# Attention and mixture-of-experts kernel on one core: eight warming matmuls, other first loads, a second task order, and register loads moved behind copies

## The chip, the cores and the metric

The kernel runs on one core of one Trainium2 chip. The metric is the device time of the whole program in microseconds (us), lower is better. Before the change it is 468.69 us, the median of 3 runs (468.49 to 468.74).

## The reference, cut to what matters

The input is q, k, v of 4 batches, 8 heads, 576 rows, 64 columns, a memory per head, and the weights of 8 experts, all in float32.

```python
scores = where(causal, -1e9, q @ k.T / sqrt(64)); a = softmax(scores); local = a @ v
phi = where(x > 0, x, exp(x) - 1) + 1
mem_out = (phi(q) @ M_prev) / (phi(q) @ z_prev + 1e-6)
x = sigmoid(beta) * mem_out + (1 - sigmoid(beta)) * local      # 2304 rows of 512
e_idx = argmax(x @ w_gate, axis=1)
for e in range(8):                                             # each row goes to one expert
    out[e_idx == e] = gate_w * eom * (relu(x @ w1[e]) @ w2[e])
```

## The kernel before, in words

**Attention.** The 32 heads are handled as 16 pairs g = 0 to 15, four pairs to a batch. A pair's q and k lie transposed in one tile `qk` (128 partitions, 1280 columns): 64 columns of q's last rows (`TQ`), then the q block, then k. Each value is split into a rounded part `hi` and the remainder `lo` (float32r), and a score block is three matmuls: hi by lo, lo by hi, hi by hi (`score`, L549). The first operand named is the stationary one and comes from q, the second from k.

A step is a pair and one of five row blocks qt. Its tasks are: SS (scores, TensorE), M (mask, scale and row minimum, VectorE, L628 and L596), E (exponential, ScalarE, L633), T (transposes, TensorE, L645), V (copy of the transposed block out of PSUM, ScalarE or VectorE, L492). Per pair there are also load and load_v (transfers, issued by SyncE), C (`hi` of a whole pair, ScalarE, L461), R (`lo` of a whole pair, GpSimd, L465), P (values, TensorE, L680), O (copy of P's result), and F0 to F2 (phi of q). Per batch there are MW and MC (memory weights), ME, N1, N2, G (memory term), PV, Y, XD, OUT (sum of both terms and its store), LT to LA (logits), RT, RK, Tgate, Tpos, SEL (routing). The last batch uses PL, YL, TL, XL instead of PV, Y and XD. Z tasks and fetch prepare the fullest expert early.

**The order of the work.** The list `ORDER` (L50) names all 1181 tasks of the attention; a loop (L1092) emits them one by one. Each engine executes its own instructions strictly in that order, so `ORDER` fixes the queue of every engine. A name with `:ACT` or `:DVE` behind it is a copy that can go to either engine.

**The start.** `warm(12)` (L941) issues twelve bf16 matmuls of 512 columns on a tile of ones, which TensorE executes while the first transfers run. `load(0)` (L429) brings pair 0 in pieces (`pieces`, L411): k columns and q columns of the first 256 rows (128 KB each), then k (160 KB) and q (192 KB) of the other rows, then TQ (32 KB). The first q piece is issued by ScalarE's queue, all others by SyncE's. `load(1)` (640 KB, L953) follows. Then `first(0)` and `first_low(0)` (L467, L474) make `hi` and `lo` of the first pieces: VectorE casts k, ScalarE casts q, VectorE subtracts q and then k. `constants()` (L194) issues the transfers of beta, wg and rzt. Tasks first1 to first3 repeat this for the second pieces: ScalarE and VectorE cast, VectorE subtracts q, GpSimd subtracts k.

**The experts.** After the attention the rows are gathered expert by expert in 17 slots of 128 rows. `gemm1` (L1441) multiplies a slot by w1, `stage_h` (L1448) transposes the result on TensorE and makes hT and hh on ScalarE and hl = hT - hh on GpSimd, and `gemm2` (L1468) multiplies by w2. A function given to `gemm1` as `mid` is emitted in the middle of its matmuls. `numbers(g0, g1)` (L1545) loads expert numbers from the tile `groupi` into ScalarE's registers; `wide_load` (L1549) uses them for the addresses of transfers that ScalarE issues. Between the experts' set-up and the slot loop stand these lines:

```python
1639    numbers(0, QUARTERS)                 # three registers
1640    gemm1(1, lambda: stage_h(0))
```

Of the kernel before, what the change touches and what calls it, by code (L numbers as in the profile page):

```python
# [54 lines left out]
T1_2_0 V1_2_0:ACT T1_2_1 M2_0_0 M2_0_1 M2_1_1 E2_0_1 TS0_0 F03 P0_256_0 V1_2_1:DVE E2_0_0 E2_1_1 T1_4 M1_3_1 F21 V1_4_0:ACT LM1 M2_1_0 M1_3_0 P0_256_1
C3:DVE F12 P1_0_0 E2_1_0 V1_4_1:DVE T2_0 load4 E1_3_0 E1_3_1 V2_0:DVE SS2_2 R3 M2_2_0 M2_2_1 O0_256:ACT O1_0:ACT SS2_3 T2_1 T1_3_1 load_v3 E2_2_0
V2_1:ACT M2_3_0 V1_3_1:ACT TS1_0 E2_3_0 SS2_4 T1_3_0 V1_3_0:ACT M2_3_1 MW1 F13 F04 E2_2_1 T2_2_0 T2_3_0 TS1_1 ranks M2_4_0 P1_256_0 C4:DVE E2_3_1 F22 MC1
V2_2_0:ACT SS3_1 M3_0_0 V2_3_0:ACT P1_256_1 T2_2_1 M3_1_0 M2_4_1 E2_4 V2_2_1:ACT E3_0_0 load5 F23 O1_256:DVE M3_0_1 T2_3_1 TS2_0 load6 E3_0_1 E3_1_0
V2_3_1:DVE SS3_2 ME0_0 M3_2_1 T2_4 E3_2_1 R4 M3_1_1 wgz V2_4_0:ACT N10_0 N20_0 V2_4_1:ACT F06 SS3_4 T3_2_1 T3_0 M3_2_0 ME0_1 F14 V3_0:ACT M3_4_0
V3_2_1:ACT SS4_1 M3_4_1 E3_2_0 N10_1 SS4_2 E3_1_1 N20_1 T3_1 T3_2_0 C5:ACT P2_0_0 P2_256_0 TS2_1 E3_4 M4_0_0 V3_1:ACT M4_0_1 F24 M4_2_1 G0_1 M4_2_0  # L60
V3_2_0:ACT O2_0:ACT E4_0_1 E4_0_0 T3_4 M4_1_1 E4_1_1 E4_2_1 P2_256_1 V3_4_0:DVE TS3_0 M4_1_0 O2_256:DVE T4_0 SS3_3 E4_1_0 load_v4 E4_2_0 V3_4_1:DVE
M3_3_0 ME0_4 C6:ACT V4_0:ACT T4_2_0 SS4_4 V4_2_0:ACT R5 N10_4 T4_2_1 R6 TS3_1 N20_4 M3_3_1 M4_4_0 V4_2_1:ACT T4_1 E3_3_0 M4_4_1 load7 E3_3_1 V4_1:ACT
ME0_3 SS4_3 E4_4 T3_3_1 V3_3_1:ACT T3_3_0 N10_3 V3_3_0:ACT N20_3 M4_3_0 F16 E4_3_0 M4_3_1 ME0_2 N10_2 TS4_0 F05 SS5_1 SS5_2 N20_2 F26 T4_4 M5_0_0
M5_0_1 E4_3_1 P3_0_0 V4_4_0:DVE P3_256_0 O3_0:ACT E5_0_0 load9 P4_0_0 E5_0_1 M5_1_0 G0_3 P3_256_1 load_v5 F15 C7:ACT M5_2_0 W0 O3_256:ACT T4_3_0
O4_0:ACT F07 V4_4_1:DVE F25 E5_1_0 R7 T4_3_1 PV0_2 M5_2_1 M5_1_1 PV0_1 SS5_4 V4_3_1:ACT E5_1_1 E5_2_1 V4_3_0:DVE T5_0 Y0_2 G0_4 V5_0:ACT E5_2_0 Y0_1
M5_4_0 SS5_3 G0_0 M5_4_1 LT0_0 load8 XD0_1 LC0_0:DVE T5_2_0 V5_2_0:ACT XD0_2 M5_3_1 T5_1 PV0_4 E5_4 M5_3_0 T5_2_1 SS6_2 SS6_1 V5_2_1:DVE F09 V5_1:ACT
E5_3_0 E5_3_1 Y0_4 OUT0_2 M6_0_0 LT0_1 F08 M6_2_1 LC0_1:ACT T5_4 load_v7 OUT0_1 E6_0_0 V5_4_0:ACT F19 M6_2_0 LM2 LS0 SS6_4 TS5_1 V5_4_1:ACT TS5_0
E6_2_1 F17 M6_1_0 TS4_1 T5_3_1 T5_3_0 LY0 XD0_4 M6_0_1 E6_0_1 LB0 G0_2 V5_3_1:ACT V5_3_0:ACT PV0_0 P4_256_0 M6_1_1 T6_2_1 F18 LA0 RT0_0 Y0_0 E6_1_1
E6_1_0 RT0_1 T6_0 SS7_1 XD0_0 P4_256_1 P5_256_0 O4_256:ACT V6_0:ACT V6_2_1:DVE M6_4_0 RT0_2 E6_2_0 C8:ACT R8 F27 RT0_3 RT0_4 M7_0_0 P5_0_0 P5_256_1
OUT0_4 T6_1 CA0 F28 E7_0_0 O5_0:ACT M6_4_1 E6_4 O5_256:DVE T6_2_0 load_v6 V6_2_0:ACT M7_0_1 M7_1_1 ME1_0 SS6_3 M7_1_0 SS7_3 load_v8 V6_1:ACT load10  # L70
E7_1_1 RX0 N11_0 E7_0_1 C9:ACT T6_4 N21_0 V6_4_0:ACT E7_1_0 PV0_3 M6_3_1 E6_3_1 M6_3_0 P6_0_0 Y0_3 V6_4_1:DVE TS6_0 E6_3_0 T7_0 O6_0:DVE M7_3_0 M7_3_1
R9 TS6_1 V7_0:ACT SS7_2 ME1_4 N11_4 E7_3_0 T6_3_1 T7_1 E7_3_1 SS7_4 V7_1:ACT N21_4 M7_2_0 Tgate10 E7_2_0 V6_3_1:ACT M7_2_1 ME1_2 G1_0 N11_2 SS8_1
T6_3_0 N21_2 F29 Tgate30 T7_3_1 V6_3_0:ACT V7_3_1:ACT C10:ACT MW2 MC2 M7_4_0 T7_3_0 M8_0_0 OUT0_0 E7_2_1 M8_0_1 load11 M7_4_1 ME1_1 XD0_3 T7_2_1 N11_1
N21_1 V7_3_0:ACT T7_2_0 E8_0_0 R10 SS8_2 E7_4 M8_1_1 ME1_3 M8_1_0 V7_2_1:ACT V7_2_0:ACT E8_0_1 E8_1_1 M8_2_0 Tgate20 F011 T7_4 OUT0_3 load13 SS8_3
# [16 lines left out]
P11_256_1 M12_4_1 SEL1_2 T12_1 M13_0_0 T12_3_1 M13_1_0 O11_256:ACT M13_0_1 V12_1:ACT M13_1_1 E12_4 XD2_1 PV2_4 PV2_3 R14 Y2_4 E13_1_1 T12_3_0 E13_0_1
SS12_2 SS13_3 XD2_4 OUT2_1 OUT2_4 V12_3_1:ACT V12_3_0:DVE M12_2_1 G2_4 E13_1_0 GA1 E13_0_0 T12_4 Y2_3 V12_4_0:ACT E12_2_1 F014 LT2_0 M12_2_0 LT2_1
T13_0 F012 SEL1_1 XD2_3 V12_4_1:DVE T13_1 LC2_0:DVE LC2_1:ACT V13_0:DVE M13_3_0 LS2 E12_2_0 V13_1:ACT SS13_2 T12_2_0 T12_2_1 E13_3_0 V12_2_1:ACT LY2
P12_0_0 M13_3_1 TS12_0 SEL0_4 load_v13 V12_2_0:ACT M13_2_0 O12_0:ACT PV2_0 LB2 M13_2_1 E13_2_0 SS13_4 T13_3_0 PV2_2 Y2_0 F112 F114 T13_2_0 Y2_2
# [1709 lines left out]
```

## Time and profile before

| what | value |
|---|---|
| median of 3 runs | 468.69 us (468.49 to 468.74) |
| the profiled execution's own time | 468.34 us |
| its span, first to last instruction | 466.3 us |
| instructions | 10798 |
| TensorE busy | 456.7 us (98% of the span) |
| VectorE, ScalarE, GpSimd busy | 284.9, 262.4, 271.1 us |

The span is what the trace covers; the profiled execution's own time is 2.0 us longer. A busy TensorE is not a TensorE at its peak, since a matmul that is held up counts as busy while it is pipelined. In the trace PE is TensorE's matmuls, PEld its weight loads, DVE VectorE, ACT ScalarE, POOL GpSimd, SP SyncE, and a q behind a name is that engine's sequencer, which issues transfers. An idle stretch in square brackets is followed by what ended it.

### The profile page before, as it was taken

What the parts mean: (1) busy time and instruction counts of PE and PEld (TensorE: products, weight loads), DVE (VectorE), ACT (ScalarE), POOL (GpSimd) and SP (SyncE); (2) the same over time, 40 slices, a digit from 0 to 9 for tenths busy, and PEclk for the clock granted to TensorE, in tenths of its full rate; (3) what the DMA queues carried; (4) which work ended last, traced back from release to release, by engine and by line L of the source; (5) the groups of instructions that cost most, each with busy time, mean ns of one, the idle gap of its engine ahead of it and who ended that gap; (6) DMA issues with size and microseconds to landing.
All of it is one profiled execution on the core that took longest, in us unless ns stands there. A gap on an engine that the chain in (4) does not pass through costs nothing.

```text
span 466.3 us, 10798 instructions
## 1 busy us (share of the span) xinstructions
PE 456.7 (98%) x3517; PEld 354.8 (76%) x3517; DVE 284.9 (61%) x851; ACT 262.4 (56%) x625; POOL 271.1 (58%) x274
## 2 busy tenths in 40 slices
...
GB/s 239 204 144 143 21 216 158 158 58 199 30 153 30 86 181 99 59 142 153 47 265 324 299 309 170 328 46 346 265 202 341 115 208 221 124 147 182 29 31 39
DMA packets 30119, 75.90 MB, mean 163 GB/s; under 512 B 4307, under 2 KB 4839, under 8 KB 30058
## 3 DMA queue, kind: packets, MB, share of 16 engines
...
## 4 chain that ended last, share of the span: by engine, by line
PE 88%; DVE 3%; issue 2%; POOL 2%; ACT 2%; DVEq 1%; POOLq 0%; ACTq 0%
PE py L1432 18%; PE h L1432 17%; PE po L680 10%; PE pt L645 8%; PE s L570 7%; PE me L736 4%; PE hp L1458 3%; PE cy L1601 3%; PE ch L1601 3%; PE sd L557 3%; PE pt L614 2%; PE px L1400 2%; PE he L1123 1%; PE pv L799 1%; PE pl L904 1%
## 5 line engine op out<-in xcount | busy, mean ns | idle before, releaser
L633 ACT ACTIVATE st<-st,nm 128x128 f32<-128x128 f32 (+3 forms) x128 | 71.4, 562 | 3.7 <-DVE nm L628 3.6
L1465 POOL TENSOR_TENSOR hl<-hT,hh 128x512 fp32r<-128x512 f32 x32 | 43.5, 1380 | 40.6 <-ACT hh L1464 40.5
L628 DVE CUSTOM_DVE_ANT_0 st<-s,mask 128x128 f32<-128x128 f32 (+3 forms) x128 | 58.2, 483 | 8.2 <-PE s L570 4.1
L1108 DVE CAST whi<-kept 128x1024 fp32r<-128x1024 f32 x32 | 26.0, 811 | 51.6 <-ACTq L1439 40.7
L465 POOL TENSOR_TENSOR lo<-qk,hi 128x1216 fp32r<-128x1216 f32 x15 | 42.1, 2805 | 24.7 <-ACT hi L461 19.5
L1111 DVE TENSOR_TENSOR wlo<-kept,whi 128x1024 fp32r<-128x1024 f32 x32 | 54.4, 1701 | 1.1
L492 ACT COPY PT<-pt 128x512 f32<-128x512 f32 (+2 forms) x89 | 45.2, 523 | 15.9 <-PE pt L645 13.8
L1432 PE MATMUL h<-whi,xh 128*128 (+1 forms) x136 | 53.9, 396 | 0.0
L1432 PE MATMUL h<-whi,xl 128*128 (+1 forms) x136 | 53.4, 393 | 0.0
L1432 PE MATMUL h<-wlo,xh 128*128 (+1 forms) x136 | 53.4, 392 | 0.0
L1432 PE MATMUL py<-whi,hh 128*128 (+1 forms) x128 | 51.9, 406 | 0.0
L1432 PE MATMUL py<-whi,hl 128*128 (+1 forms) x128 | 50.2, 392 | 0.3 <-POOL hl L1465 0.3
L1432 PE MATMUL py<-wlo,hh 128*128 (+1 forms) x128 | 50.2, 392 | 0.0
L680 PE MATMUL po<-PT,v 128*64 128x320 f32 (+4 forms) x480 | 49.1, 349 | 0.8 <-ACT oT_hT L492 0.4
L645 PE MATMUL pt<-ident,st 128*128 128x128 f32 x320 | 48.0, 280 | 0.4 <-ACT st L633 0.4
L1464 ACT CAST hh<-hp 128x512 fp32r<-128x512 f32 x32 | 19.1, 598 | 50.6 <-PE py L1432 50.6
L1445 ACT ACTIVATE h<-h 128x1024 f32<-128x1024 f32 x17 | 17.5, 1029 | 47.9 <-PE h L1432 47.9
L680 PEld LDWEIGHTS po<-PT,v 128*64 128x64 f32 x480 | 29.6, 137 | 17.7 <-issue 2.8
L1411 POOL TENSOR_TENSOR xl<-x,xh 128x512 fp32r<-128x512 f32 x16 | 21.7, 1358 | 34.3 <-issue 19.0
L645 PEld LDWEIGHTS pt<-ident,st 128*128 128x128 f32 x320 | 35.2, 142 | 7.8 <-ACT st L633 2.5
...
L1432 PEld LDWEIGHTS h<-whi,xh 128*128 128x128 f32 x136 | 25.5, 188 | 6.0 <-ACT h L1445 0.3
...
## 6 DMA issues: line engine op xcount, KB each, us to landing
...
```

Source lines behind the costliest of these rows:

```text
L465: G.tensor_tensor(c["lo"][:, TQ:], c["raw"][:, TQ:], f32(c["hi"])[:, TQ:], op=ALU.subtract)
L492: (A.copy if e == "ACT" else V.tensor_copy)(dst(), src())
L570: T.matmul(c()["ss", q][j], l[r, lc], m[r, KC:KC + w], start=(a == 0), stop=(a == 2))
L628: V.tensor_tensor_reduce(st[:, :w], c()["ss", qt][j], mask[:, 512 - w:512], -SCALE, 3.0e38, ALU.add, ALU.min, negm()[:, i:i + 1])
L633: A.activation(st, st, AF.Exp, bias=c()["negm"][:, i:i + 1], scale=-1.0, accum_out=sums()[:, qt, 2 * p + j:2 * p + j + 1])
L645: T.transpose(pt[:, (m * k1 + i) * P:(m * k1 + i + 1) * P], st[:, i * P:(i + 1) * P], ident)
L680: T.matmul(po[64 * j:64 * j + 64, qs - q0:q1 - q0], vt[:, k, 64 * j:64 * j + 64], PT[:, j, k, qs:q1], start=(k == 0), stop=(k == kn - 1))
L1108: join((A.copy if eng is A else eng.tensor_copy)(whi[:, e % 2, c, :], raws[e, c]))
L1111: join(eng.tensor_tensor(wlo[:, e % 2, c, :], raws.pop((e, c)), f32(whi[:, e % 2, c, :]), op=ALU.subtract))
L1432: i = T.matmul(o[n % nh], l[:, z], m[:, n * 512 + part.start:n * 512 + part.stop], start=(c == 0 and k == 0 and n < nh), stop=(c == 3 and ...
L1465: G.tensor_tensor(hl[:, z], hT[:, z], f32(hh)[:, z], op=ALU.subtract)
L1601: i = apart(T.matmul(o[w * q:w * q + w], x[:, z:z + w], wide[b][:, m + size * q:m + size * q + size], start=(j == 0), stop=(j == len(todo) ...
```

## The change

Four things are changed. `warm` issues eight matmuls instead of twelve. At the start, the second q piece of pair 0 is issued by ScalarE's queue instead of SyncE's, `load(1)` is issued behind beta and wg instead of ahead of them, rzt behind the memory's tiles mz and mt instead of ahead of v, and `first_low(0)` subtracts k ahead of q. `ORDER` is another list of the same 1181 tasks, with other engines for 57 of its 184 copies. `numbers(0, QUARTERS)` is emitted inside `gemm1(1, ...)`, behind the copies of `stage_h(0)`, instead of ahead of `gemm1(1, ...)`.

The diff, with `ORDER` cut to its first lines behind the common start and to its last lines:

```diff
 ORDER = """
...
-E0_3_1 V0_1:DVE F10 M0_2_0 SS0_4 T0_3_0 M0_2_1 T0_3_1 load2 R1 V0_3_0:DVE MW0 E0_2_0 T0_2_0 M0_4_0 E0_2_1 V0_3_1:ACT MC0 M0_4_1 F01 SS1_1 SS1_2 M1_0_0
-T0_2_1 M1_1_0 V0_2_0:ACT F20 E0_4 V0_2_1:DVE M1_1_1 load3 C2:ACT fill0 M1_0_1 E1_0_0 load_v2 R2 P0_0_0 E1_1_0 E1_1_1 M1_2_0 load_v1 F02 T0_4 E1_0_1
...
-E15_3_1 W3_1_3 O14_256:ACT YLl1_1 XLl2_0 PLl4_1 PLl3_0 YLl4_1 GP0 T15_3_0 TL1_1 V15_3_0:ACT XLl1_1 XLl4_1 TL4_1 YLl3_0 PLl0_1 T15_3_1 GS0 RT2_0 GO0
-RT2_1 RT2_2 RT2_3 GP1 T15_2_0 YLl0_1 RT2_4 Tgate12 GS1 V15_3_1:ACT OL4 RX2 GO1 RK2 V15_2_0:ACT CA2 Tpos12 Tgate32 Tpos22 Tgate22 CJ2 T15_2_1 Tpos32
...
+E0_3_1 V0_1:DVE F10 M0_2_0 SS0_4 T0_3_0 M0_2_1 T0_3_1 load2 V0_3_0:DVE M0_4_0 E0_2_0 R1 MW0 MC0 M0_4_1 T0_2_0 SS1_1 E0_2_1 F01 M1_1_1 V0_3_1:ACT
+V0_2_0:DVE E0_4 M1_1_0 T0_2_1 E1_1_1 F20 M1_0_0 P0_0_0 V0_2_1:ACT load3 SS1_2 C2:ACT M1_0_1 E1_1_0 E1_0_1 fill0 load_v2 T0_4 R2 load_v1 F02 V0_4_0:DVE
...
+T15_3_1 PLl0_1 GS0 RT2_0 GO0 V15_3_0:ACT RT2_1 T15_2_0 RT2_2 V15_3_1:DVE RT2_3 T15_2_1 V15_2_0:ACT GP1 YLl0_1 RT2_4 G3_3 Tgate12 GS1 OL4 RX2 GO1 RK2
+CA2 Tpos12 V15_2_1:ACT Tgate32 Tpos22 Tgate22 CJ2 Tpos32 P15_384_0 Tgate42 GA2 CB2 Tgate52 P15_256_0 Tpos42 Tgate62 TL0_1 O15_384:ACT TL3_0 XLl3_0
...
@@ constants()
         SY.dma_start(wg, wgo)
-        SY.dma_start(rzt, rz)
@@ load(g), g == 0
                 SY.dma_start(c["raw"][:, zk], qk[b, p, :, zk])
-                (SY if i else A).dma_start(c["raw"][:, zq], qk[b, p, :, zq])
+                A.dma_start(c["raw"][:, zq], qk[b, p, :, zq])
@@ first_low(n, ez)
-        for z, eng in zip(pieces(n), (V, ez)):
+        for z, eng in list(zip(pieces(n), (V, ez)))[::1 if n else -1]:
@@ the start
-    warm(12)
+    warm(8)
...
-    load(1)
     first(0)
     first_low(0)
     constants()
+    load(1)
     SY.dma_start(xs[MID:MID + 1], maskd[0:1, :DM])
...
     load_v(0)
     load_mem(0)
+    SY.dma_start(rzt, rz)
@@ ahead of the slot loop
-    numbers(0, QUARTERS)
-    gemm1(1, lambda: stage_h(0))
+    gemm1(1, lambda: (stage_h(0), numbers(0, QUARTERS)))
```

## Rows read from the trace of the kernel before

**Rows 1.** The page: shares of the chain that ended last, by engine
```profile
PE 88%; DVE 3%; issue 2%; POOL 2%; ACT 2%; DVEq 1%; POOLq 0%; ACTq 0%
```

**Rows 2.** Busy time by stretch: length, then PE, PEld, DVE, ACT, POOL, clock, DMA
```profile
6.00:60.00 54.00, 53.28 (x515) 41.73 (x516) 46.44 (x169) 48.75 (x140) 36.31 (x46) 1.00 0.46 155
60.00:130.00 70.00, 70.00 (x705) 55.76 (x703) 61.97 (x235) 61.16 (x168) 44.03 (x46) 1.00 0.38 129
130.00:200.00 70.00, 68.78 (x696) 54.09 (x692) 60.62 (x249) 49.52 (x146) 33.07 (x45) 1.00 0.32 100
```

**Rows 3.** TensorE at the start: start, duration, instruction (second row: a narrower window)
```profile
1.12 4.87 PE L192 MATMUL warm<-ones 128*128 128x512 bf16 x12 [1.12 <-DVE ones L940]
5.37 0.63 PE L192 MATMUL warm<-ones 128*128 128x512 bf16 x2
5.93 0.39 PE L570 MATMUL s<-lo,hi 64*128 64x256 f32 x2
...
6.67 0.45 PE L570 MATMUL s<-lo,hi 64*128 64x512 f32 x2
```

**Rows 4.** The other engines at the start, same columns; then a window with GB/s last
```profile
0.94 0.41 ACTq L437 DMA_DIRECT2D qk<-in_qk  x1
3.51 0.41 ACT L472 CAST hi<-qk 128x256 fp32r<-128x256 f32 x1 [1.21 <-DMA qk<-in_qk]
5.58 0.51 ACT L472 CAST hi<-qk 128x384 fp32r<-128x384 f32 x1 [1.66 <-DMA qk<-in_qk]
...
3.15 0.29 DVE L472 CAST hi<-qk 128x256 fp32r<-128x256 f32 x1 [2.08 <-DMA qk<-in_qk]
3.94 0.76 DVE L477 TENSOR_TENSOR lo<-qk,hi 128x256 fp32r<-128x256 f32 x2 [0.50 <-ACT hi L472]
6.12 0.56 DVE L477 TENSOR_TENSOR lo<-qk,hi 128x384 fp32r<-128x384 f32 x1 [1.18 <-ACT hi L472]
6.98 0.29 DVE L628 CUSTOM_DVE_ANT_0 st<-s,mask 128x128 f32<-128x128 f32 x1 [0.30 <-PE s L570]
...
3.00:3.50 0.50, 0.50 (x3) 0.15 (x1) 0.29 (x1) 0.00 (x0) 0.45 (x3) 1.00 0.87 316
```

**Rows 5.** SyncE's queue and ScalarE's next whole-pair cast: start, duration, instruction
```profile
1.73 0.43 SPq L437 DMA_DIRECT2D qk<-in_qk  x1
...
2.68 0.47 SPq L440 DMA_DIRECT2D qk<-in_qk  x1
...
8.64 0.33 SPq L440 DMA_DIRECT2D qk<-in_qk  x1
...
9.09 1.19 ACT L461 CAST hi<-qk 128x1216 fp32r<-128x1216 f32 x1
```

**Rows 6.** What TensorE waited for, whole span: us in total, times, longest
```profile
PE po L680 <- ACT oT_hT L492: 0.4, 1, 0.4
```

**Rows 7.** Timeline around the second slot's first product, 227 to 234 us
```profile
227.26 0.20 DVE L1314 TENSOR_REDUCE groupi<-ohe 128x5 int32<-128x40 f32 x1
...
227.61 1.03 PE L1458 MATMUL hp<-ident,h 128*128 128x128 f32 x8
...
229.79 0.59 ACT L1463 COPY hT<-hp 128x512 f32<-128x512 f32 x1 [3.22 <-DVE hit L1187]
...
230.95 3.17 POOL L1465 TENSOR_TENSOR hl<-hT,hh 128x512 fp32r<-128x512 f32 x2 [2.78 <-ACT hh L1464]
...
231.70 1.07 ACT L1445 ACTIVATE h<-h 128x1024 f32<-128x1024 f32 x1
...
232.16 0.48 PE L1432 MATMUL py<-whi,hh 128*128 128x512 f32 x1
...
232.91 0.50 PE L1432 MATMUL py<-whi,hl 128*128 128x512 f32 x1 [0.28 <-POOL hl L1465]
...
233.25 0.39 PE L1432 MATMUL py<-wlo,hh 128*128 128x512 f32 x1
233.49 0.40 PE L1432 MATMUL py<-whi,hh 128*128 128x512 f32 x1
```

More of the change, by code (lines that the diff above doesn't have):

```diff
@@ L55 @@
[L55 to L74, printed above, removed]
@@ L91 @@
[L91 to L94, printed above, removed]
@@ new lines @@
+T2_2_0 V2_2_0:ACT TS2_0 ME0_0 E3_0_1 T2_4 load6 R4 V2_4_0:ACT N10_0 SS3_4 V2_4_1:ACT T3_2_1 N20_0 M3_2_0 M3_4_0 T3_0 M3_1_0 ME0_1 E3_1_1 wgz
+V3_2_1:ACT V3_0:ACT M3_4_1 N10_1 E3_1_0 N20_1 SS4_1 SS4_2 E3_2_0 T3_1 F06 F14 M4_0_0 T3_2_0 C5:ACT M4_1_1 P2_256_0 V3_2_0:ACT M4_1_0 E3_4 V3_1:ACT
+G0_0 TS2_1 F24 TS3_0 M4_0_1 P2_0_0 P2_256_1 O2_0:DVE E4_1_0 O2_256:ACT E4_0_0 M4_2_1 E4_0_1 T3_4 E4_2_1 ME0_4 SS3_3 M4_2_0 N10_4 V3_4_0:ACT N20_4
+V3_4_1:ACT load_v4 T4_0 SS4_4 E4_1_1 E4_2_0 T4_1 M3_3_0 V4_0:ACT C6:ACT R5 M3_3_1 M4_4_0 V4_1:ACT T4_2_0 ME0_3 E3_3_1 SS4_3 T3_3_1 E3_3_0 V4_2_0:DVE
@@ new lines @@
+N10_3 N20_3 T4_2_1 ME0_2 M4_4_1 V3_3_1:ACT R6 E4_4 G0_4 SS5_2 TS3_1 load7 M4_3_0 T3_3_0 F16 TS4_0 F05 M4_3_1 N10_2 N20_2 F26 V4_2_1:ACT SS5_1 load9
+V3_3_0:ACT T4_4 P3_0_0 O3_0:DVE M5_2_1 P3_256_0 load_v5 E4_3_1 F15 C7:ACT V4_4_0:ACT V4_4_1:ACT E4_3_0 W0 M5_1_1 E5_1_1 P4_0_0 P3_256_1 E5_2_1
+O4_0:DVE T4_3_1 F07 M5_0_1 M5_0_0 T4_3_0 M5_1_0 F25 PV0_1 O3_256:ACT SS5_4 V4_3_1:ACT V4_3_0:ACT E5_0_0 PV0_2 M5_2_0 T5_2_1 G0_2 Y0_1 R7 M5_4_0 E5_0_1
+SS5_3 LT0_0 V5_2_1:ACT E5_2_0 load8 Y0_2 M5_4_1 T5_2_0 XD0_1 E5_1_0 LC0_0:DVE XD0_2 T5_1 V5_2_0:ACT F09 M5_3_0 M5_3_1 E5_4 PV0_4 OUT0_2 Y0_4 T5_0
@@ new lines @@
+XD1_2 T8_3_1 M9_2_0 T9_1 SS9_4 V8_3_1:ACT LC1_0:DVE LC1_1:DVE M9_3_1 LS1 TS8_0 XD1_3 V9_1:ACT T8_4 M9_2_1 E9_3_0 M9_4_0 SS10_1 LY1 PV1_4 E9_3_1 LB1
+OUT1_3 RK0 Tpos10 M9_4_1 V8_4_0:ACT OUT1_2 Y1_4 LA1 RT1_0 RT1_1 V8_4_1:ACT E9_2_1 T9_3_1 Tpos20 T9_3_0 M10_1_1 C12:ACT P8_256_0 P8_0_0 Tpos30
+V9_3_0:ACT M10_1_0 Tpos40 V9_3_1:ACT M10_0_0 E10_1_1 E10_1_0 P8_256_1 RT1_2 E9_4 T9_2_1 T10_1 SS10_2 CB0 O8_0:DVE M10_0_1 O8_256:ACT E10_0_1 SS10_3
+V10_1:ACT ME2_0 V9_2_1:ACT E9_2_0 T9_2_0 F213 RT1_3 RT1_4 M10_2_0 M10_3_0 N12_0 N22_0 E10_0_0 TS9_1 T10_0 V9_2_0:ACT V10_0:ACT SS10_4 R12 T9_4 ME2_3
@@ new lines @@
+load_v11 RX1 M10_2_1 E10_2_0 M10_4_0 V9_4_0:DVE N12_3 E10_2_1 SS11_1 N22_3 SEL0_3 E10_3_0 V9_4_1:ACT T10_3_0 SEL0_2 ZI T10_2_1 TS9_0 C13:ACT R13
+P9_256_0 M11_0_0 M10_4_1 E11_0_0 P9_0_0 M11_0_1 M10_3_1 V10_3_0:ACT O9_0:DVE V10_2_1:ACT P9_256_1 XD1_4 E10_3_1 O9_256:ACT T10_3_1 E10_4 TS8_1 load15
+T10_2_0 M11_1_1 E11_1_1 V10_3_1:DVE M11_1_0 ME2_1 SS11_3 V10_2_0:ACT OUT1_4 F015 N12_1 SS11_4 N22_1 E11_1_0 Tgate11 Tgate31 T10_4 SEL0_1 RK1 MW3
+E11_0_1 V10_4_0:ACT T11_1 M11_3_0 Tpos11 M11_4_0 load14 TS10_1 MC3 V10_4_1:ACT M11_4_1 Tpos21 T11_0 ME2_4 SS11_2 M11_3_1 CA1 E11_4 SS12_1 N12_4
@@ new lines @@
+V11_1:ACT V11_0:ACT N22_4 CJ1 T11_4 M12_1_1 CB1 V11_4_0:ACT ZC P11_0_0 E11_3_0 TS11_1 Z1 Z2 Tpos31 O11_0:ACT load_v12 E11_3_1 Z3 M12_0_1 Z4 E12_1_1
+P10_256_0 V11_4_1:DVE P10_0_0 G2_4 Z5 TS11_0 F115 P10_256_1 Tpos41 Z6 M12_1_0 Z7 Tgate21 T11_3_1 Z8 E12_1_0 E12_0_1 M11_2_0 T11_3_0 O10_0:DVE Z9
+O10_256:ACT M11_2_1 ME2_2 SS12_3 Z10 V11_3_1:ACT M12_0_0 TS10_0 E11_2_0 V11_3_0:DVE E11_2_1 ZN T11_2_0 C14:ACT N12_2 T11_2_1 E12_0_0 Tgate41 N22_2 W2
+V11_2_1:ACT M12_3_1 V11_2_0:ACT SEL1_3 SS12_4 PV2_1 load_v14 Y2_1 F215 T12_1 M12_4_0 V12_1:ACT E12_3_1 T12_0 P11_256_0 M12_3_0 M12_4_1 SEL1_4
@@ new lines @@
+P11_256_1 SS13_1 V12_0:DVE M13_0_0 M13_1_1 SEL1_2 E12_3_0 T12_3_0 O11_256:ACT XD2_1 PV2_4 M13_0_1 R14 Y2_4 T12_3_1 E12_4 E13_0_0 XD2_4 SS13_3 G2_1
+V12_3_0:ACT V12_3_1:ACT OUT2_1 OUT2_4 GA1 G2_2 T12_4 E13_0_1 PV2_3 V12_4_0:ACT F014 LT2_0 T13_0 M13_3_1 M13_3_0 SS12_2 Y2_3 LT2_1 F012 SEL1_1 M13_1_0
+XD2_3 E13_3_0 M12_2_0 SS13_2 E13_1_0 LC2_0:DVE LC2_1:ACT V12_4_1:DVE M12_2_1 E12_2_0 E13_1_1 LS2 V13_0:ACT LY2 TS12_0 T12_2_0 SS13_4 G2_0 M13_2_0
+PV2_0 E12_2_1 T12_2_1 V12_2_0:ACT Y2_0 SEL0_4 M13_4_0 T13_1 P12_0_0 V12_2_1:ACT O12_0:ACT P12_256_0 load_v13 M13_2_1 PV2_2 T13_3_0 LB2 E13_2_0
```

56 lines of the change are left out of this document (28 added, 28 removed).

## The prediction

> **What bounds the kernel now.** I read the chain that ended last first. TensorE holds 88% of it [rows 1], so what counts is work that TensorE does, and stretches in which it does none. The table of stretches then says where the second kind lies. From 6 to 60 us TensorE is busy 53.28 of 54.00 us, from 60 to 130 us all 70.00, from 130 to 200 us 68.78 of 70.00 [rows 2]. In 194 us of attention TensorE is idle 0.72 + 0 + 1.22 = 1.94 us; the granted clock is 1.00 throughout. VectorE and ScalarE, busy 61.97 and 61.16 us of the 70 in the middle, follow it closely but don't hold it up. So no order of the same tasks can win more than these 1.94 us, and what moves the end otherwise is when the attention begins and what lies behind it.
>
> The timeline of the start shows when it begins. Twelve warming matmuls run from 1.12 to 5.99 us, and the first score matmul follows at 5.93, without a gap. Ten of them start before 5.37, so their pitch is (5.37 - 1.12) / 10 = 0.425 us for 512 columns, the half clock of 1.2 GHz. The last two share 5.93 - 5.37 = 0.56 us, 0.28 each: the engine rises to 2.4 GHz there, near 5.4 us, after 4.3 us of unbroken matmuls [rows 3].
>
> The other engines' rows show what the scores wait for if the warming ends earlier. VectorE casts the first k at 3.15, ScalarE the first q at 3.51 to 3.92, and VectorE subtracts only at 3.94, after 0.50 us idle behind ScalarE: two subtractions, 0.76 us, done at 4.70. The second q piece arrives last: ScalarE waits 1.66 us for it, until 5.58, VectorE subtracts it at 6.12 to 6.68, and only then, at 6.98, comes the first row minimum [rows 4], from which all of the attention's M and E follow.
>
> **The change, part by part.**
>
> *Warming and first loads.* Eight warming matmuls end at 1.12 + 8 x 0.425 = 4.52 us instead of 5.93: 1.41 us that TensorE gets back, if the scores are ready. With k subtracted first, VectorE uses its idle 0.50 us: k's remainder from 3.44 to 3.82, q's from 3.94 to 4.32 [rows 4]. That is 0.2 us ahead of 4.52; in the old order 4.70 would have been 0.2 us late. But the clock is still half at 4.52. The first score block takes 6.67 - 5.93 = 0.74 us at full clock [rows 3]. If the clock rises where it does now, 0.9 us at half clock do 0.45 us of it, the other 0.29 run at full clock, and the block ends near 5.71 instead of 6.67: a gain of 0.96 us, 0.45 given back.
>
> The next thing due is the second q piece. It is issued third on SyncE now, at 1.73 [rows 5], and lands 5.58 - 1.73 = 3.85 us later by ScalarE's wait. Afterwards ScalarE's queue issues it right behind the first, whose issue takes 0.94 to 1.35 and whose data ScalarE uses at 3.51, 2.57 us after its issue [rows 4]. From 1.35, with the same 2.57 us and 0.6 us for 192 KB at the 316 GB/s of that stretch [rows 4], I get 4.5; cast until 5.0, subtracted until 5.6, row minimum after the score block's end at about 6.0 instead of 6.98: the same gain of 1.0.
>
> The Trainium skill speaks against this piece: its page "DMA: Bandwidth & Descriptors", section "Issuing engines are not separate DMA queues", says that transfers end on the same 16 engines whoever issues them, and that another issuer saves only issue time. By that rule the piece would gain 1.73 - 1.35 = 0.38 us and the front about 0.4 instead of 1.0. I don't take it, because the same edit also sends the 640 KB of `load(1)` off its path, as the next rows show.
>
> `load(1)` is issued at 2.68 now, 0.95 us behind the second q piece on the same queue, and while that piece is still under way [rows 5]. Afterwards SyncE issues k, k, TQ, beta, wg and then `load(1)`: one issue less and two more ahead of it, 2.68 + 0.47 = 3.15. What waits for it is ScalarE's cast of the whole of pair 1, at 9.09 now, about 8.1 afterwards, with all later E tasks queued behind it and GpSimd's R1 waiting. `load(1)` has landed by 8.64 now, where SyncE's next load is released [rows 5]. If it lands 0.47 later than that, the cast stalls up to 1.0 us and the front's gain is gone; if it gains from the 192 KB that no longer run beside it, there is no stall. I take the second, as the second q piece is the larger part of what shared with it. Moved past on SyncE are also xs, v, mz and mt, earlier or unchanged, and rzt, first used by wgz far into the attention: nothing. Front: **-1.0**, between 0 and -1.41.
>
> *The second order.* Counted in the two lists: 295 TensorE tasks with 118 changes of array mode in both, GpSimd's and SyncE's lists the same word for word, no TensorE task more than ten places from where it was, and 57 copies on the other engine (ScalarE's 136 of 184 become 139). It is the same schedule, shaken. TensorE's work is equal, so only waits differ: at best -1.94. The largest single wait is 0.4 us, a value product behind a copy out of PSUM [rows 6]. In the new tail P14_256 stands between the last pair's products, and both T15_2 stand ahead of GP1 and RK2, so TensorE has work where it waited for copies and the routing. I take **-0.2**; each new wait costs about 0.4, so three net ones give +1.2, the other end.
>
> *The registers.* `groupi` is written at 227.26 to 227.46; behind it ScalarE's three register loads fill its sequencer until hT's copy at 229.79, though the transposes that the copy reads ended at 227.61 + 1.03 = 228.64. The copies, then hl on GpSimd at 230.95, are late by 1.1 us, and TensorE's second product matmul starts at 232.91. From the first, at 232.16, with the pitch 233.49 - 233.25 = 0.24, it would start at 232.40: 0.51 us lost [rows 7]. With the copies first, hl starts near 229.9, its first half (3.17 / 2 = 1.6 us) ends near 231.5, and nothing waits. The register loads now lie ahead of relu at 231.70: if they start with the copies at 228.7, their 2.3 us end at 231.0; if they wait for the copies' end, relu comes about 1.2 us late, and TensorE meanwhile has the twelve product matmuls and more. hl may slow VectorE's last subtractions, which have slack too. **-0.5**, between 0 and -0.7.
>
> **Sum.** 0.2 + 0.5 + 1.0 = 1.7 us. The profiled execution's own time of 468.34 becomes 466.6; it lies 0.35 below the median of the runs, so against 468.69 I forecast **467.0**. A difference of 0.2%, 0.94 us, is about what a measurement of this kernel can tell from no change.
>
> **The rivals.**
>
> *The front gives little.* The second q piece or `load(1)` lands late, as priced above: front -0.3, registers -0.5, 467.9. For it: SyncE waits for `load(1)` until 8.64 [rows 5]; against it: it lost its largest neighbour. The rule on issuers above would give this case too. Chance 0.18.
>
> *The clock rises late.* Today's rise came after 4.3 us of unbroken matmuls [rows 3]; now there are 3.4, and then small score blocks. If TensorE stayed at 1.2 GHz until about 9 us, the matmuls between 5.71 and 9, at most 3.3 us, would take twice as long; I take 1.9 of it, since a part falls into waits that exist anyway: 467.0 + 1.9 = 468.9. The Trainium skill's page "TensorE: Matmul & The Clock Gate", Part 1, says that the array starts at half rate and that activity releases it; rows 3 agree. Against it: scores follow at once at 4.52. Chance 0.08.
>
> *The new order waits, and the kernel is slower.* TensorE takes its tasks strictly in order, so one late copy holds all. Pair 12 is the place: T12_2_0 stands three TensorE tasks behind its scores, where its average is eleven, and P12_256 two behind its last transposes. This and similar places must cost 2.64 us, six to seven waits of 0.4 [rows 6], before it decides; with nine it is 469.6 or so. Against it: the old list has leads of three too (T3_2_1), and no wait of its lasts over 0.4 us [rows 6]. Chance 0.12.
>
> *The new order closes the gaps.* 1.5 instead of 0.2 of the 1.94 us: 465.7. Chance 0.12.
>
> **How the numbers follow.** The forecast keeps 0.50, with its own range from 466.2 to 467.7. Faster: 0.50 + 0.12 = 0.62; the same: 0.18 + 0.08 = 0.26; slower: 0.12. The range from 465.6 to 468.9 leaves out the slower case and the edges.
>
> **What would show it.** In the changed kernel the first score matmul stands at 4.5 us with half-clock pitch, ScalarE's second q cast at 4.5, the first row minimum near 6.0, pair 1's cast at 8.1 without a wait; TensorE's idle time between 6 and 200 us is no more than 1.94; hT follows the transposes directly, and no product matmul waits for hl. A late cast of pair 1, weight loads far apart after 5.5 us, or waits of TensorE around pair 12 would make the prediction wrong.

## The result and the profile after

The changed kernel takes 472.31 us, the median of 4 runs (472.14 to 472.82), against 468.59 us for the kernel before in the same session: a ratio of 1.0078 [1.0064, 1.0091]. It is 3.7 us slower, the forecast was 467.0 us, and 472.31 lies outside the range. The profiled execution took 472.19 us, with a span of 470.5 us.

The chain that ended last, by engine, answers to [rows 1]; VectorE's share is 5% where it was 3%:

```profile
PE 89%; DVE 5%; ACT 2%; issue 2%; POOL 1%; POOLq 0%; DVEq 0%
```

The stretches of [rows 2] in the changed kernel (length, then PE, PEld, DVE, ACT and POOL with their instructions, clock, DMA share, GB/s):

```profile
6.00:60.00 54.00, 53.27 (x505) 41.27 (x504) 46.02 (x161) 48.12 (x133) 39.93 (x45) 1.00 0.45 155
60.00:130.00 70.00, 67.70 (x656) 52.73 (x658) 64.15 (x225) 60.43 (x168) 38.50 (x43) 1.00 0.38 125
130.00:200.00 70.00, 69.38 (x703) 54.36 (x699) 59.55 (x244) 50.33 (x149) 36.64 (x46) 1.00 0.30 99
```

In the middle stretch TensorE had no idle time before; now it has 2.30 us. In the same stretch it starts 656 matmuls instead of 705, while VectorE is busy 2.18 us longer with 10 instructions fewer. An engine that does less in more busy time is being held inside its instructions.

What TensorE waited for between 5 and 235 us, its four largest rows (us in total, times, longest), where [rows 6] had 0.4 as its longest:

```profile
PE pv L798 <- DVE oT_h L491: 1.0, 1, 1.0
PE sd L556 <- DVE nm L627: 0.9, 1, 0.9
PE rk L234 <- DVE oha L269: 0.7, 1, 0.7
PE po L679 <- DVE gs L311: 0.6, 1, 0.6
```

All four name VectorE. The start of the changed kernel answers to [rows 3 to 5] (start, duration, instruction):

```profile
1.12 3.59 PE L192 MATMUL warm<-ones 128*128 128x512 bf16 x8 [1.12 <-DVE ones L939]
...
4.55 0.51 ACT L471 CAST hi<-qk 128x384 fp32r<-128x384 f32 x1 [0.56 <-DMA qk<-in_qk]
...
4.65 0.58 PE L569 MATMUL s<-lo,hi 64*128 64x256 f32 x2
...
5.09 1.01 DVE L476 TENSOR_TENSOR lo<-qk,hi 128x384 fp32r<-128x384 f32 x1 [0.41 <-ACT hi L471]
...
6.34 0.29 DVE L627 CUSTOM_DVE_ANT_0 st<-s,mask 128x128 f32<-128x128 f32 x1 [0.23 <-PE s L569]
...
8.44 1.19 ACT L460 CAST hi<-qk 128x1216 fp32r<-128x1216 f32 x1
```

The scores start 1.28 us earlier, the first row minimum 0.64 us (6.98 to 6.34). ScalarE's cast of the second q piece stands at 4.55 instead of 5.58, and pair 1's cast at 8.44 shows no wait.

To see where the rest went I compare, task by task, when TensorE reaches the same task in both traces. At 15 us the changed kernel is 0.7 us ahead, at 58 us 0.5 us. Then it falls back in four jumps: 1.7 us between 58 and 66 us, 1.3 near 80, 1.6 between 118 and 125, 0.7 between 202 and 206. At the experts' first transposes it is 4.63 us late (227.61 before [rows 7], 232.24 after). At each jump one VectorE instruction lasts far too long, and each time it starts just behind one of GpSimd. Changed kernel, timeline around the four places (VectorE's instruction, then GpSimd's):

```profile
56.84 2.72 DVE L766 SCALAR_TENSOR_TENSOR rr<-sums,gc 128x40 f32<-128x40 f32 x1
...
56.73 2.77 POOL L464 TENSOR_TENSOR lo<-qk,hi 128x1216 fp32r<-128x1216 f32 x1 [0.16 <-ACT hi L460]
...
77.71 3.10 DVE L519 SCALAR_TENSOR_TENSOR phi<-qk,phi 128x576 f32<-128x576 f32 x1
...
77.40 2.79 POOL L464 TENSOR_TENSOR lo<-qk,hi 128x1216 fp32r<-128x1216 f32 x1 [1.89 <-ACT hi L460]
...
121.78 2.56 DVE L269 SCALAR_TENSOR_TENSOR oha<-mx,wt 128x40 bf16<-128x40 f32 x1
...
120.95 3.33 POOL L464 TENSOR_TENSOR lo<-qk,hi 128x1216 fp32r<-128x1216 f32 x1
...
207.73 1.23 DVE L269 SCALAR_TENSOR_TENSOR oha<-mx,wt 128x40 bf16<-128x40 f32 x1
...
207.49 1.42 POOL L922 TENSOR_TENSOR xa<-x,yl 128x256 f32<-128x256 f32 x2
```

The same first pair in the kernel before:

```profile
58.14 0.19 DVE L767 SCALAR_TENSOR_TENSOR rr<-sums,gc 128x40 f32<-128x40 f32 x1
...
59.38 2.85 POOL L465 TENSOR_TENSOR lo<-qk,hi 128x1216 fp32r<-128x1216 f32 x1 [2.91 <-ACT hi L461]
```

The instruction W0, `rr`, is 40 columns wide and takes 0.19 us when it runs 1.2 us ahead of the subtraction R7. When it comes up 0.11 us behind R7's start it takes 2.72 us and ends (59.56) just behind R7 (59.50). The other three also end just behind their GpSimd instruction, at most 0.7 us (the `phi` step, which takes 0.74 us by itself). What they have in common is two operands in SBUF; a VectorE operation with one operand in PSUM is not held: in the changed kernel with the old order, copies and row minima of normal length run all through these subtractions. The Trainium skill's page "SBUF — State Buffer", section "Who interferes with whom", states the rule: a VectorE instruction with two SBUF inputs contends with a GpSimd instruction that reads SBUF, and the later one blocks until the first has ended. The four rows agree, to 0.1 us at W0. But the rule is wider than what these traces show. GpSimd's own step of phi (F0) reads `qk` in SBUF too, as its only tensor, and VectorE's `phi` steps run through it at their normal 0.75 us each. Changed kernel:

```profile
99.84 1.65 POOL L512 TENSOR_SCALAR phi<-qk 128x576 f32<-128x576 f32 x1
...
100.38 1.42 DVE L519 SCALAR_TENSOR_TENSOR phi<-qk,phi 128x576 f32<-128x576 f32 x2
```

Over the traces of all runs, the steps of this kind that start inside a GpSimd `phi` take 0.74 to 1.09 us, their median is 0.75, and those that start inside a GpSimd subtraction of a whole pair take 1.31 to 3.12. So it is GpSimd's instructions with two operands in SBUF that hold VectorE here; why the others don't is open.

### The profile page after: what moved, and what is told of

It is laid out like the page before. It is cut to its first block, busy times and chain, and to the rows that moved or that the text cites. A ratio compares the mean times of both kernels' runs of the same rounds, so it can differ in the third digit from the quotient of the medians.

```text
span 470.5 us, 10798 instructions
## 1 busy us (share of the span) xinstructions
PE 457.5 (97%) x3513; PEld 354.4 (75%) x3513; DVE 291.1 (62%) x848; ACT 263.8 (56%) x628; POOL 272.8 (58%) x274
## 4 chain that ended last, share of the span: by engine, by line
PE 89%; DVE 5%; ACT 2%; issue 2%; POOL 1%; POOLq 0%; DVEq 0%
PE h L1432 20%; PE py L1432 18%; PE po L679 9%; PE pt L644 7%; PE s L569 6%; PE me L735 4%; PE hp L1458 3%; PE cy L1601 3%; PE ch L1601 3%; PE sd L556 2%; PE px L1400 2%; ACT st L632 2%; PE pt L613 2%; PE pye L1140 1%; PE pv L798 1%
## 5 line engine op out<-in xcount | busy, mean ns | idle before, releaser
L632 ACT ACTIVATE st<-st,nm 128x256 f32<-128x256 f32 (+3 forms) x128 | 71.4, 561 | 15.2 <-DVE nm L627 13.5
L1108 DVE CAST whi<-kept 128x1024 fp32r<-128x1024 f32 x32 | 27.8, 869 | 51.5 <-ACTq L1439 40.0
L491 ACT COPY PT<-pt 128x512 f32<-128x512 f32 (+2 forms) x93 | 46.9, 521 | 15.0 <-PE pt L644 11.7
L1111 DVE TENSOR_TENSOR wlo<-kept,whi 128x1024 fp32r<-128x1024 f32 x32 | 53.2, 1662 | 1.1
L512 POOL TENSOR_SCALAR phi<-qk 128x576 f32<-128x576 f32 x16 | 27.0, 1696 | 6.1 <-DMA qk<-in_qk 4.3
```

The lines of the kernel that those rows point to most:

```text
L491: (A.copy if e == "ACT" else V.tensor_copy)(dst(), src())
L632: A.activation(st, st, AF.Exp, bias=c()["negm"][:, i:i + 1], scale=-1.0, accum_out=sums()[:, qt, 2 * p + j:2 * p + j + 1])
L1108: join((A.copy if eng is A else eng.tensor_copy)(whi[:, e % 2, c, :], raws[e, c]))
L1111: join(eng.tensor_tensor(wlo[:, e % 2, c, :], raws.pop((e, c)), f32(whi[:, e % 2, c, :]), op=ALU.subtract))
```

## The experiments

Theory A: the holds of VectorE by GpSimd are the loss, and the new order makes them only by letting these tasks meet. Rival B: the order costs by its other waits, and a stretched instruction only fills time that is lost anyway. Times are medians; the kernel before had 468.83, 468.95 and 469.07 us in the three sessions (experiments 1 to 4, 5 to 8, 9 to 11).

**1. The change without the new order.** `ORDER` is the old list, the rest as changed.

```diff
-ORDER = """ the new list """
+ORDER = """ the list of before """
```

> The changed kernel with the order of before: eight warming matmuls, the new first loads and the moved register loads are kept. Theory A (the loss is in the new order: three two-operand instructions of VectorE start just behind a whole-pair subtraction of GpSimd and are held until it ends): no such hold, the front's gain of 0.65 us and the registers' 0.53 us remain, so 468.6 - 1.2 = 467.4 (467.0 to 467.9). Theory B (the new start itself costs later on, by its loads or the late clock): 470 or more. Theory C (any order planned for another start is shaken into such holds): 469 to 473, with a VectorE instruction of over 2 us in the trace.

Measured: 467.42 us (9 runs, 466.99 to 467.9), ratio 0.9969 [0.9959, 0.9979]. In the attention VectorE has no long hold: W0 runs ahead of R7 again (timeline, VectorE's instruction, then GpSimd's).

```profile
57.13 0.18 DVE L766 SCALAR_TENSOR_TENSOR rr<-sums,gc 128x40 f32<-128x40 f32 x1
...
58.38 2.85 POOL L464 TENSOR_TENSOR lo<-qk,hi 128x1216 fp32r<-128x1216 f32 x1 [2.91 <-ACT hi L460]
```

TensorE keeps a lead of 1.02 us over the kernel before from 15 us to the end of the attention, and of 1.58 us from the register loads on, of which 1.25 are left at 400 us. So the order costs 4.9 us, and without it the change is faster than before.

**2. The new order alone**, in the kernel before.

> The kernel before with the new order alone: twelve warming matmuls, the old first loads, the old place of the register loads. Theory A: the new order carries its holds along, 468.6 + 4.9 = 473.5 (472 to 474.5), with W0, F2 of pair 7 and the routing of batch 1 each over 2 us on VectorE. Theory B: no loss from the order, about 468.6. Theory C: the holds depend on the timing, so some of the three are gone and others may have come, 468 to 472.

Measured: 473.85 us (4 runs), ratio 1.0106 [1.0089, 1.0123]. The holds travel with the order: `rr` from 57.78 to 60.51, `phi` from 78.65 to 81.77, `oha` from 122.73 to 125.28, `oha` of batch 2 at 208.70. (The second is the last step of pair 8's exponentials, not of pair 7's as the expectation says.) TensorE reaches the experts' first transposes 5.6 us late.

**3. The register loads alone**, in the kernel before.

```diff
-    numbers(0, QUARTERS)
-    gemm1(1, lambda: stage_h(0))
+    gemm1(1, lambda: (stage_h(0), numbers(0, QUARTERS)))
```

> The kernel before with the register loads moved behind the copies, nothing else. All theories: 468.6 - 0.5 = 468.1, TensorE's second product matmul right behind its first. Rival: the relu behind the register loads comes late and gives the gain back: 468.6.

Measured: 468.39 us, ratio 0.9992 [0.998, 1.0005]; the interval includes no change. The trace shows the gain where it was expected: TensorE gains 0.56 us between the first transposes and the second product's matmuls, as in experiment 1 (0.55) and in the changed kernel (0.55).

**4. GpSimd behind VectorE, first attempt.** In the changed kernel GpSimd copies one column of VectorE's result before the subtraction that had held it; in `ORDER`, R8 moves one place, behind F27.

```diff
+    late = const.tile([P, 1], F32, name="late")
+    behind = {7: lambda: bs[0]["rr"][:, 0, 0:1], 8: lambda: pr[7]["phi"][:, 0:1], 12: lambda: oha[:, 1, 0, 0:1]}
     def rest(g):
         c = pr[g]
+        if g in behind:
+            G.tensor_copy(late, behind[g]())
```

> The changed kernel in which GpSimd's subtractions of pairs 7, 8 and 12 start only behind the VectorE instruction that each of them held (a small GpSimd copy of that instruction's output stands ahead of each). Theory A: the three holds are gone, 472.3 - 4.3 = 468.0 (467.2 to 468.8), less up to 0.5 if a subtraction that comes 0.4 to 1.2 us later is itself waited for. Rival (TensorE's waits come from the order of TensorE's and ScalarE's tasks, and VectorE's long instructions only fill them): 471.5 to 472.5.

Measured: 472.34 us (5 runs, 471.6 to 475.16), ratio 1.0083 [1.0055, 1.0112]. By the time alone A would have failed. The trace shows two things. The holds of `rr` and of the first `oha` are gone, and TensorE's delay at the experts' first transposes falls from 4.63 to 1.95 us (0.4 of these 1.95 come from the start, where pair 1's cast waits 0.45 us for `load(1)` in this trace); the third stays, since the guard waits for pair 7's `phi` and it is pair 8's that is held (76.73 to 79.85). And the experts, in which nothing was changed, take about 3 us longer. Experiments 5 and 8 separate the two.

**5. GpSimd behind VectorE, corrected.** The second guard waits for pair 8's `phi`, for which R8 moves behind F28 in the list, and the copies go into an existing tile, `which`.

```diff
+    behind = {7: lambda: bs[0]["rr"][:, 0, 0:1], 8: lambda: pr[8]["phi"][:, 0:1], 12: lambda: oha[:, 1, 0, 0:1]}
...
+            G.tensor_copy(which, behind[g]())
```

> The changed kernel with the new order, in which GpSimd copies one column behind each of three VectorE instructions before it starts the whole-pair subtraction that had held that instruction: R7 behind W0's division (rr), R8 behind the last step of the exponentials of pair 8 (phi; the one that the trace of the changed kernel shows held, which the run before this one missed), R12 behind the last routing step of batch 1 (oha). The copies go into a tile that exists already, so that no later tile moves. Theory A (three long holds of VectorE by GpSimd's subtractions make most of the 4.63 us by which the changed kernel is behind at the expert stage): all three stretches fall below 0.5 us, TensorE reaches the expert stage about 4 us earlier than in the changed kernel, and the time falls from 472.3 to about 468.3 (467.6 to 469.3). Rival B (the order itself, its other waits, costs the time, and the holds only fill it): the holds go, but waits elsewhere take their place, and the time stays within 1 us of 472.3. The rest of the difference to 467.4 (the changed kernel with the old order), some 0.9 us, would by A be the fourth hold (1.2 us, last routing step of batch 2) and the short waits.

Measured: 468.27 us (10 runs, 467.31 to 470.11), ratio 0.9991 [0.9975, 1.0007]: 4.0 us below the changed kernel with the same order. That the median is the 468.3 of A to the digit is luck: five runs lie between 467.3 and 467.6 us, five between 468.9 and 470.1, and the median falls in the gap. Either group contradicts B. The three instructions are short again, each with GpSimd's copy waiting for it. Guarded kernel, timeline around two of the three places:

```profile
56.71 0.20 DVE L770 SCALAR_TENSOR_TENSOR rr<-sums,gc 128x40 f32<-128x40 f32 x1
...
57.40 0.19 POOL L467 COPY which<-rr 128x1 f32<-128x1 f32 x1 [0.95 <-DVE rr L771]
57.54 2.78 POOL L468 TENSOR_TENSOR lo<-qk,hi 128x1216 fp32r<-128x1216 f32 x1
...
118.73 0.20 DVE L269 SCALAR_TENSOR_TENSOR oha<-mx,wt 128x40 bf16<-128x40 f32 x1
...
119.07 0.18 POOL L467 CAST which<-oha 128x1 f32<-128x1 bf16 x1 [1.25 <-DVE oha L269]
119.21 2.80 POOL L468 TENSOR_TENSOR lo<-qk,hi 128x1216 fp32r<-128x1216 f32 x1
```

Here GpSimd sits idle 0.95 and 1.25 us, at no cost that the trace shows. One other step, a `phi` at 59.63, now meets R7 and takes 1.31 us instead of 0.73. TensorE reaches the experts' first transposes at 227.43 instead of 232.24. Against experiment 1 (226.58) 0.85 us are left. Of these 0.67 arise between 202 and 206 us, where the fourth instruction, unguarded, still takes 1.24 us instead of 0.20; that the hold makes them was not tested. The only trace is of a run of 467.32 us, so what differs in the slower group is not shown.

**6. Three small additions inside subtractions**, in the kernel of experiment 1, where the order has no holds.

```diff
+    job("D", "DVE", 100, 0.0, lambda: V.tensor_tensor(which, ident[:, 0:1], ident[:, 1:2], op=ALU.add))
-... M5_2_1 M5_1_1 ... M7_4_1 ... M10_3_0 ...
+... M5_2_1 D M5_1_1 ... D M7_4_1 ... D M10_3_0 ...
```

> The changed kernel with the old order (467.4), in which VectorE has three more instructions, each an addition of two columns of 128 by 1 in SBUF that nothing waits for, placed in its queue so that each comes up 0.2 to 0.9 us behind the start of one of GpSimd's whole-pair subtractions (pairs 7, 10 and 12). Theory A (an instruction of VectorE with two inputs in SBUF that comes up during such a subtraction waits until it ends, whatever its size, and VectorE's queue with it): each takes 2.0 to 2.6 us instead of under 0.2 and some 7 us of VectorE go in all; in the changed kernel 8 us of holds became 5.3 us of TensorE's delay, so about 0.65 of 7: 4.6 us, 472.0 (469.5 to 474). Rival B (holds as such are absorbed; the order's other moves cost the time): 467.4 to 468.

**7. The same three additions a little earlier.**

```diff
-... F25 ... M7_4_0 ... M10_2_1 ...
+... D F25 ... D M7_4_0 ... D M10_2_1 ...
```

> The same three additions in the same kernel, but each one to three places earlier in VectorE's queue, where by the trace it comes up 0.5 to 0.8 us before the subtraction starts. Theory A: each takes under 0.2 us, together under 0.5 us, and the time is 467.4 to 467.9. If three more instructions and not the holds are what costs, the time is that of the kernel with the additions inside, which is what B would say if both rise alike.

Measured: 476.49 us inside (4 runs, 476.43 to 477.58; ratio 1.0167 [1.0148, 1.0186]) and 467.32 us outside (5 runs, 467.01 to 467.5; 0.9964 [0.995, 0.9978]): 9.2 us between the same instructions in two places. Inside, timeline of the additions and the subtractions, then two windows (PE, PEld, DVE, ACT, POOL, clock):

```profile
59.29 1.99 DVE L1075 TENSOR_TENSOR which<-ident 128x1 f32<-128x1 f32 x1
...
58.42 2.83 POOL L464 TENSOR_TENSOR lo<-qk,hi 128x1216 fp32r<-128x1216 f32 x1 [2.91 <-ACT hi L460]
...
91.88 2.55 DVE L1075 TENSOR_TENSOR which<-ident 128x1 f32<-128x1 f32 x1
...
91.66 2.76 POOL L464 TENSOR_TENSOR lo<-qk,hi 128x1216 fp32r<-128x1216 f32 x1 [4.78 <-ACT hi L460]
...
125.12 2.51 DVE L1075 TENSOR_TENSOR which<-ident 128x1 f32<-128x1 f32 x1
...
124.83 2.78 POOL L464 TENSOR_TENSOR lo<-qk,hi 128x1216 fp32r<-128x1216 f32 x1
```

```profile
97.00:100.40 3.40, 3.40 (x17) 2.20 (x15) 2.56 (x11) 2.07 (x7) 3.34 (x4) 0.51 0.00 0
...
131.00:134.50 3.50, 3.50 (x22) 2.75 (x24) 1.75 (x7) 1.04 (x3) 3.09 (x2) 0.51 0.01 2
```

Outside, the first and the last:

```profile
58.17 0.13 DVE L1075 TENSOR_TENSOR which<-ident 128x1 f32<-128x1 f32 x1
...
118.54 0.15 DVE L1075 TENSOR_TENSOR which<-ident 128x1 f32<-128x1 f32 x1
```

One column per partition, whose result nothing waits for, blocks VectorE 2 to 2.6 us. B is out. A's price was too low (472.0, at most 474): against the trace of experiment 1, TensorE loses 1.7, 4.0 and 4.1 us for holds of 1.99, 2.55 and 2.51. The windows show why the last two cost more than they last: TensorE's granted clock falls to 0.51 behind each, the level of 1.2 GHz, for 3.4 us, after TensorE had been idle 1.55 us between 91 and 97 us and 1.90 between 124 and 131. Half the clock for 3.4 us takes up to 1.7 us more; within these two stretches TensorE falls 1.4 and 1.5 us further behind, which about covers the excess of 1.5 and 1.6. Behind the first hold, with 0.66 us idle between 58 and 64, the clock stays at 1.00.

**8. A tile of 4 bytes that nothing uses**, in the kernel of experiment 1, as the first guarded kernel had one.

```diff
     sizes = const.tile([P, E], F32, name="sizes")
+    pad = const.tile([P, 1], F32, name="pad")
```

> The changed kernel with the old order (467.4) and one more tile of 4 bytes per partition that nothing writes or reads, allocated ahead of the attention's tiles, as the copies of the earlier guarded kernel had one; the tiles of the experts' halves whi and wlo move by 32 bytes. No instruction changes. In the guarded kernel the 512-column matmuls of the experts started every 233.4 ns instead of every 229.1. Theory C (where whi and wlo lie sets that pitch): 233.4 ns here too; some 816 matmuls by 4.3 ns is 3.5 us, so 470.9 (470.0 to 471.6). Rival D (the guards, or that chip in that run, made the slower pitch): 229.1 ns and 467.4 (466.9 to 468.0).

**9. The same tile with 64 bytes** (`[P, 16]`).

> As the run with the tile of 4 bytes, but the unused tile has 64 bytes per partition, so that whi and wlo move by 64 bytes instead of 32. Theory C (their place within a stretch of 64 bytes sets the pitch of the experts' matmuls): the pitch is 229.1 ns again and the time that of the kernel without the tile, 467.4 (466.9 to 468.0). Rival D (any tile more, or any move away from the present place, costs it): some 233 ns and 470.0.

Measured: 470.02 us (10 runs; 2.6 above experiment 1, at the low end of what C gave) and 469.42 us (10 runs; 2.0 above). The view by tile of the matmuls h<-wlo,xh of the experts (their number; duration min/median/max in ns; first and last start), first experiment 1, then 4 bytes, then 64 bytes:

```profile
L1432 PE MATMUL h<-wlo,xh x120: 388/394/401, 239.0 to 446.5; 128*128 x120
```

```profile
L1433 PE MATMUL h<-wlo,xh x120: 389/399/399, 239.5 to 449.5; 128*128 x120
```

```profile
L1433 PE MATMUL h<-wlo,xh x120: 390/394/405, 239.9 to 449.4; 128*128 x120
```

From the first to the last of the same 120 matmuls it is 207.5, 210.0 and 209.5 us, with not one instruction changed. The pitch of consecutive 512-column matmuls is 229.1, 233.4 and 232.5 ns on average. Experiments 5 to 7, of the same session as the 4 bytes, have the pitch of experiment 1, so it was not the chip. So where `whi` and `wlo` lie does set that pitch (the stationary operands come from pools on the other side of SBUF, which this tile does not move), and it explains the experts' loss in experiment 4; but a move by 64 bytes does not bring 229.1 back, so Theory C's "place within 64 bytes" is wrong and D's "any move away" stands as far as two moves can tell. What in the address matters is open.

**10. Twelve warming matmuls**, in the kernel of experiment 1.

```diff
-    warm(8)
+    warm(12)
```

> The changed kernel with the old order (467.4) and twelve warming matmuls again instead of eight; loads and register reads as in the changed kernel. Theory A (what the front gives, it gives by eight warming matmuls instead of twelve: TensorE is free when the first pieces are there): the first scores start 0.4 to 1.3 us later, according to when the clock rises, and the time is 467.7 to 468.5. Rival B (the first loads on ScalarE's queue give it): 467.4, within 0.3.

**11. The front alone**: the changed kernel with the old order and the register loads where they were.

> The kernel before with the front alone: eight warming matmuls, the first loads and the turned order of the second pieces, but the old order of the tasks and the register loads where they were. In four traces with this front TensorE was 0.65 to 1.03 us ahead of before from 15 us on, the more the earlier its clock rose. Theory A (the front's gain is carried to the end): 467.9 (467.6 to 468.3), so 0.6 to 1.0 below before, and with the 0.55 of the register loads it makes up what the old order in the changed kernel gained. Rival B (the gain is made of the register loads and of chance in when the clock rises): 468.4 or more.

(The order that is turned is that of the first pieces.)

Measured: 467.20 us (5 runs, 466.63 to 467.87) with twelve, 467.53 us (5 runs, 467.07 to 467.75; ratio 0.9964 [0.995, 0.9978]) with the front alone. Twelve warming matmuls are no worse than eight in these runs. The first scores start at 5.10 us instead of 4.35, but the 512-column scores start at 5.87 against 5.81: in experiment 1 TensorE waits 0.45 us ahead of them for GpSimd's remainder of the second k piece. In both traces the clock had risen early: the twelve took 4.04 us, where they took 4.87 before the change [rows 3]. And the changed kernel's 512-column scores, at half clock, start at 5.99 without a wait, so there TensorE itself came last. So that the loads give all of the front's gain is shown for an early rise alone; what the twelve cost with a late one has no trace.

The front alone is 1.5 us faster than before in its session, and its trace carries a lead of 1.02 us from 15 us to the experts. That experiment 1, with the registers' 0.55 us besides, is only 0.1 us faster lies within the spread of both.

The lead is not the same in every run. Ten traces have these first loads; in eight TensorE is 0.65 to 1.03 us ahead of the kernel before at 16 us, in experiments 4 and 9 only 0.37 and 0.19. In these two ScalarE's cast of pair 1 waits for `load(1)`, as the prediction's first rival had it. Experiment 9:

```profile
8.99 1.21 ACT L461 CAST hi<-qk 128x1216 fp32r<-128x1216 f32 x1 [0.46 <-DMA qk<-in_qk]
```

The fastest version measured is the change with the old order: 467.42, and 467.20 with twelve warming matmuls. They can't be told apart, nor from the front alone (467.53), and all three beat the two kernels.

## Why the prediction was wrong

**The front** (forecast -1.0, between 0 and -1.41): right in size. 1.0 us is what the traces of experiments 1 and 11 carry through the attention, some 0.7 that of the changed kernel. The number is no firmer than some 0.3 us: experiment 3's trace, with the old front, is itself 0.30 us behind the one before from the start on. The second q piece came as worked out (4.5 forecast, 4.55 measured), and `load(1)` held nothing up in the changed kernel, though it did in two of ten traces. The first row minimum came at 6.34 instead of 6.0. Wrong, where the clock rises early, was the share of the warming matmuls: they free TensorE, but what it does next waits for the second pieces anyway (experiment 10). One cost I had missed is of the kind that sank the rest: VectorE's remainder of the second q piece takes 1.01 us instead of 0.56 [rows 4], as it now overlaps GpSimd's remainder of the second k piece. In experiment 1 it ends at 6.17 and the second of the 512-column score matmuls starts at 6.22; in the changed kernel, at half clock, nothing waits for it.

**The registers** (-0.5): right. In the changed kernel, from 232 us:

```profile
232.24 1.03 PE L1458 MATMUL hp<-ident,h 128*128 128x128 f32 x8
233.37 0.59 ACT L1463 COPY hT<-hp 128x512 f32<-128x512 f32 x1 [2.17 <-PE hp L1458]
...
236.79 0.48 PE L1432 MATMUL py<-whi,hh 128*128 128x512 f32 x1
237.11 0.40 PE L1432 MATMUL py<-whi,hl 128*128 128x512 f32 x1
237.35 0.39 PE L1432 MATMUL py<-wlo,hh 128*128 128x512 f32 x1
```

hT's copy follows the transposes by 0.10 us, and the second product matmul no longer waits for hl. The third comes 5.11 us behind the transposes, 5.64 before [rows 7]: 0.53 gained.

**The second order** (-0.2, between -1.94 and +1.2): this is the step that failed. It measured about +5 us: 4.9 between experiment 1 and the changed kernel, 5.0 between experiment 2 and the kernel before. I priced a new wait at 0.4 us, the largest that TensorE had in the kernel before [rows 6], and took three of them as the upper end. That row could show only waits that the old order had left. It was an order from which the long collisions were missing, so no row of its waits could price one. The prices stood elsewhere in the same trace: the subtraction R7 lasts 2.85 us, and W0 runs 1.2 us ahead of it. A short collision stood there too: the fourth place, batch 2's `oha`, takes 0.55 us before the change, where the other batches' take 0.20, because it comes up during a two-operand instruction of GpSimd.

```profile
203.78 0.55 DVE L270 SCALAR_TENSOR_TENSOR oha<-mx,wt 128x40 bf16<-128x40 f32 x1
...
203.54 0.73 POOL L923 TENSOR_TENSOR xa<-x,yl 128x256 f32<-128x256 f32 x1
```

I counted GpSimd's list as "the same word for word" and took it for harmless. But the holds arise between two queues: GpSimd's stayed in order while VectorE's tasks moved against it, W0 by 1.35 us from ahead of R7 to 0.11 us behind its start.

**The rivals.** "The new order waits, and the kernel is slower" had the sign, with a chance of 0.12 and 469.6 us. Its mechanism was another one: copies that come late around pair 12, at 0.4 us each. The holds are at four other places and last 1.2 to 3.1 us. The clock did not stay low until 9 us, but in the changed kernel it rose near 7 us instead of 5.4: its first 512-column score matmuls start at 5.99, 6.52 and 6.95, those of before at 6.67, 6.96 and 7.19. `load(1)` was not late there; in experiments 4 and 9 it was. The gaps were not closed: between 6 and 200 us TensorE is idle 3.65 us (0.73 + 2.30 + 0.62) instead of 1.94, and that is not all of the loss, since a matmul that is held up counts as busy. For the same reason the 1.94 us were no firm bound on what an order can win.

What should have warned me is also in the kernel: it marks W0, the `phi` steps and the routing steps `port=True`. I read the two lists for distances on TensorE's queue and not for which of these tasks stands next to which R.
